# Group 0's softmax probabilities taken to their partitions by identity matmuls and ScalarE copies instead of a DMA round trip, with another hand-out order

## The chip, the cores and the metric

One NeuronCore of one Trainium2 chip. The metric is the device time of one execution in microseconds (us). TensorE is called PE, VectorE DVE, ScalarE ACT, GpSimd POOL and the queue of SyncE SP, as in the profile.

## The reference

A transformer block on one sequence of 2048 tokens with 512 features: an adaptive layer norm, sliding dilated attention, a residual, a second adaptive layer norm, a gated feed-forward part (1792 wide) and a residual.

```python
mod = silu(c) @ w_mod                       # six rows of 512: sa, ca, ga, sb, cb, gb
h = layernorm(x) * (1 + ca) + sa
q, k, v = split(h @ wqkv)                   # 32 heads of 16
off = arange(8) * 2                         # each token sees itself and 7 earlier ones, every second
logits[s, w] = q[s] . k[s - off[w]] * 16 ** -0.5    # -1e9 where s < off[w]
attn = softmax(logits, over w)
o[s] = sum_w attn[s, w] * v[s - off[w]]
x = x + ga * (o @ wo)
h = layernorm(x) * (1 + cb) + sb
x = x + gb * ((gelu(h @ w_gate) * (h @ w_up)) @ w_down)
```

## The kernel before

**Tiling.** The 2048 tokens are four groups (sg 0 to 3) of 512, each of four chunks of 128. A group goes through: `ln1` (statistics on DVE and ACT, `rstd` on POOL, normalised `x0` to `x3` on DVE), a transpose on PE or by DMA (`t1`, `transp`, L439) and its evacuation with scale and shift (`h0` to `h3` on ACT, L486); `qkv` (L543), twelve blocks `qp.sg.blk.j` of four matmuls of 128x512, evacuated by ACT as casts `qkv.sg.blk.j` (L567 to L571; blk 0 is q, 1 is k, 2 is v); the attention; `x1` (output projection and residual); `ln2`; and the feed-forward part (`g`, `u`, `gl`, `ub`, `hh`, `y`, `ot`).

**Attention.** q and k lie with features on partitions: partition 4h + d' holds head h, and j = 0 to 3 counts four slices of the 16 features. `pq.sg.j` (DVE, L616) multiplies q by the eight shifted k; `lp.sg.j` (PE, L630) sums over the features with the 0/1 matrix `M`, using the array in four quarters of 32 columns (`tile_position=(0, 32*g)`), so that the logits `LT` lie with partition = (chunk g, head) and [8 offsets, 128 tokens]. The softmax follows there (`soft`, L638): `mx` (DVE), `z` (DVE), `e` (ACT, exp), `s1`, `ri`, `p` (DVE). The result `B["e", sg]`, bf16, is kept as [w pair a, t, 128 tokens] per partition.

The second half of the attention needs the probabilities on other partitions: `PT`, one partition per (head, a), with [t, 512 tokens]. `pt_dma(sg)` (L684) does that through memory: `est.sg` stores `e` to `escr`, and `pt.sg.0`, `pt.sg.1` load it back, all on SP. The values v go through memory too: `vst.sg` stores vT, four loads `V4.sg.0` to `V4.sg.3` (L598) bring them back with two shifted rows per offset. Then `pv.sg.j` (DVE, L705) multiplies PT by V, `o.sg.j` (PE, L719) sums over the offsets with `M` in quarters again, `oT.sg.j` (ACT, L730) evacuates, and `x1p` (PE, L740) projects.

**What sets the order.** Every operation is an `Op` of a named thread (one generator each): engine, a cost in us for the planner, the function that emits it, names it comes `after`, buffers it takes and gives back, and its name `fire`. `ORDER` (L18) is a list of 872 thread numbers; the kernel emits the next operation of the thread that stands there. Each engine runs its operations in the order in which they are emitted, and waits at the head of its queue. PSUM is divided into four `mm` buffers (projection and feed-forward results), two `att` buffers (transposes, `o`, `x1`) of a bank each, and `lg`, two banks for the logits. Weights and group inputs are issued on SP in that order too, and `LN1.3.t` is a DMA transpose on SP (L454), whose result ACT evacuates as `LN1.3.h0` to `h3`.

Of the kernel before, what the change touches and what calls it, by code (L numbers as in the profile page):

```python
# [15 lines left out]
NEG = -4.0e9  # L16

ORDER = [  # L18
# [34 lines left out]
]  # L53


# [49 lines left out]
def kernel(  # L105
# [45 lines left out]

    ident = const.tile([P, P], BF16, name="ident")
    M = const.tile([P, H], BF16, name="Mph")
    maskT = const.tile([H, W, 16], F32, name="maskT")
    neghalf = const.tile([P, 4], F32, name="neghalf")
    modT = const.tile([P, 8], F32, name="modT")
# [20 lines left out]
    def setup():  # L177
        def f0():
            make_identity(nc, ident[:])
            nc.gpsimd.memset(neghalf[:], -0.5)  # L180
        yield Op("POOL", 0.9, f0, fire="ident")

        def f1():
            nc.gpsimd.memset(M[:], 1.0)
            nc.gpsimd.affine_select(out=M[:], in_=M[:], pattern=[[-4, H]], compare_op=ALU.is_ge, fill=0.0, base=0,
                                    channel_multiplier=1)
            nc.gpsimd.affine_select(out=M[:], in_=M[:], pattern=[[4, H]], compare_op=ALU.is_ge, fill=0.0, base=3,
                                    channel_multiplier=-1)
            nc.gpsimd.memset(maskT[:], 0.0)
            for w in range(1, W):  # L190
                nc.gpsimd.memset(maskT[:, W - 1 - w, 0:2 * w], NEG)
        yield Op("POOL", 2.5, f1, fire="consts")

        yield Op("POOL", 0.2, lambda: nc.gpsimd.memset(kT[:, :, 0:16], 0.0), fire="k0")

    def warmup(cold, n):
        yield Op("DVE", 0.25, lambda: nc.vector.memset(gB[:], 0.0), fire="warm")
# [386 lines left out]
    def vload(sg):  # L584
        if sg < NSG - 1:
            yield Op("POOL", 0.2, lambda: nc.gpsimd.tensor_copy(out=vh[:], in_=B["vT", sg][:, :, SG:VR]),  # L586
                     after=[f"qkv.{sg}.2.3"], fire=f"vh.{sg}")

        def f():
            nc.sync.dma_start(out=vscr[sg][:], in_=B["vT", sg][:])  # L590
        yield Op("SP", 0.65, f, after=[f"qkv.{sg}.2.3", f"vz.{sg}"], give=[SL["vs"]], fire=f"vst.{sg}", lat=1.1)
        n = 4 * VR
        for i in range(4):
            def f(i=i):
                if i == 0:
                    B["V4", sg] = T("v4", [P, 4, 4, VR], BF16, "V4")
                src = bass.AP(vscr[sg].tensor, vscr[sg].offset + i * n + 2, [[4 * n, H], [2, 4], [1, n - 8]])
                nc.sync.dma_start(out=_ap(B["V4", sg][:, i, 0, :], [[1, n - 8]]), in_=src)  # L598
            yield Op("SP", 0.65, f, after=[f"vst.{sg}"], take=[SL["v4"]] if i == 0 else [], fire=f"V4.{sg}.{i}", lat=1.6)

# [78 lines left out]
    def exp_table():  # L679
        for sg in (2, 3):  # L680
            yield Op("ACT", 0.15, lambda: nc.scalar.activation(out=junk[:], in_=neghalf[:], func=ACT.Exp), act="exp",
                     fire=f"pre.{sg}")

    def pt_dma(sg):  # L684
        def f():
            nc.sync.dma_start(out=escr[sg][:], in_=B["e", sg][:])
        yield Op("SP", 0.65, f, after=[f"p.{sg}"], give=[SL["es"]], fire=f"est.{sg}", lat=0.4)
        for t in range(2):
            def f(t=t):
                if t == 0:  # L690
                    B["PT", sg] = smp["PT"].tile([P, 2, SG], BF16, name="PT")
                src = bass.AP(escr[sg].tensor, escr[sg].offset + t * P, [[2 * P, P], [H * W * P, CPS], [1, P]])
                nc.sync.dma_start(out=B["PT", sg][:, t, :].rearrange("p (g s) -> p g s", s=P), in_=src)
            yield Op("SP", 0.65, f, after=[f"est.{sg}"] + ([f"pv.{sg - 1}.3"] if sg else []), take=[SL["PT"]] if t == 0 else [],
                     fire=f"pt.{sg}.{t}", lat=0.6)
# [14 lines left out]
    def pv_mm(sg):  # L710
        j0 = 0
        for n in GV[sg]:
            def f(j0=j0, n=n):
                for j in range(j0, j0 + n):
                    o_ps = T("att", [P, SG], F32, "o_ps")
                    B["o", sg, j] = o_ps
                    for t in range(2):
                        for i in range(4):
                            nc.tensor.matmul(o_ps[H * i:H * i + H, :], lhsT=M[:], rhs=B["pv", sg, j][:, t, i, :],  # L719
                                             start=(t == 0), stop=(t == 1), tile_position=(0, H * i))  # L720
            yield Op("PE", 0.44 * n, f, quad=True, after=[f"pv.{sg}.{j0 + n - 1}", "consts"], take=[SL["att"]] * n, give=[SL["prod"]] * n,
                     fire=f"o.{sg}.{j0 + n - 1}")
            j0 += n

# [179 lines left out]
```

## Time and profile before

| | us |
|---|---|
| Three runs | 235.75, 238.24, 236.55 |
| Median | 236.55 |
| The profiled execution's own time | 235.66 |
| Its span, first to last instruction | 233.9 |

Busy time of the profiled execution: PE 229.1 (98%), DVE 168.2 (72%), ACT 152.5 (65%), POOL 24.3 (10%). Sizes of the moved data: `escr<-e` 256 KB a store, landing 2.2 us after its issue; `PT<-escr` 128 KB a load, 3.0.

How to read it: rows of the timeline give start, length, engine, line, operation, what is written and read, and a count; in brackets stands how long the engine idled before and what it waited for. Rows of DVE and ACT overlap a little, so the price of one in a run is the distance of two starts. Rows of the stretches give busy times by engine. A shape of `128*32` for a matmul means that it uses 32 of 128 columns of the array, and four such run side by side.

### The profile page before, as it was taken

Reading aid. Unit: us, or ns where it says so; the run is one execution under the profiler, and the core shown is the slowest. Engines: PE = TensorE matmul, PEld = TensorE weight load, DVE = VectorE, ACT = ScalarE, POOL = GpSimd, SP = SyncE. Lnnn points to the kernel's source line nnn. Section 1 sums busy time; section 2 is a strip of 40 time slices with the busy share of each in tenths; the row PEclk is TensorE's granted clock in tenths of the full one; section 3 lists DMA queues with packets and bytes.
Section 4 is the critical chain, followed back from the end, with each engine's and each line's share of the span. In section 5 each row is a group of like instructions: output and inputs, shape, how many; then the busy total and the mean of one; then the engine's idle time right before and its main releaser. Section 6 shows DMA issues by size and latency. Waiting matters only on the chain.

```text
span 233.9 us, 3653 instructions
## 1 busy us (share of the span) xinstructions
PE 229.1 (98%) x1382; PEld 106.9 (46%) x1382; DVE 168.2 (72%) x240; ACT 152.5 (65%) x284; POOL 24.3 (10%) x37
## 2 busy tenths in 40 slices
PE   7899999999999999999999999999999999999995
PEld 2755454444544344444444444444444444444443
DVE  4889999999998999999899996944852213222222
ACT  4999998877997579936786961634468631467400
POOL 3210320791200000100000010000100000000000
PEclk9999999999999999999999999999999999999999
DMA  6999776999188582045003616110023000100011
GB/s 212 386 348 241 218 301 154 266 367 396 41 266 227 209 291 82 1 92 157 22 0 100 273 45 122 38 45 0 0 47 69 0 22 22 44 4 0 0 48 45
DMA packets 30217, 30.42 MB, mean 130 GB/s; under 512 B 14840, under 2 KB 26104, under 8 KB 30200
## 3 DMA queue, kind: packets, MB, share of 16 engines
q1 hardware_dynamic: 29664, 29.67, 40.8%
q10 hardware_dynamic: 536, 0.53, 0.6%
q8 instruction: 11, 0.18, 0.3%
q14 instruction: 6, 0.05, 0.1%
HBM read 22.78 MB, written 5.31 MB: 120 GB/s over the span
## 4 chain that ended last, share of the span: by engine, by line
PE 84%; DVE 9%; DMA 3%; ACT 1%; SPq 1%; issue 0%
PE g_ps L770 21%; PE u_ps L770 21%; PE y_ps L782 19%; PE qkv_ps L553 9%; PE x_ps L740 6%; DVE pq L616 5%; PE o_ps L719 3%; DMA x<-in_A_x_dram 3%; PE LTp L630 2%; PE y_ps L793 1%; DVE xn L434 1%; DVE st L394 1%; ACT qT L567 1%; DVE e L674 1%; DVE LTp L653 1%; DVE mx L647 1%
## 5 line engine op out<-in xcount | busy, mean ns | idle before, releaser
L770 PE MATMUL g_ps<-h,Wg 128*128 128x512 bf16 x224 | 57.5, 379 | 0.0
L770 PE MATMUL u_ps<-h,Wu 128*128 128x512 bf16 x224 | 57.5, 379 | 0.0
L820 DVE TENSOR_TENSOR hht<-gl,ub 128x512 bf16<-128x512 bf16 x56 | 23.0, 420 | 33.7 <-ACT ub L809 33.5
L782 PE MATMUL y_ps<-Wd,hht 128*128 128x512 bf16 x210 | 47.0, 379 | 0.0
L809 ACT CAST ub<-u_ps 128x512 bf16<-128x512 f32 x56 | 32.9, 588 | 20.4 <-PE u_ps L770 20.4
L802 ACT ACTIVATE gl<-g_ps 128x512 bf16<-128x512 f32 x56 | 33.6, 600 | 18.4 <-PE g_ps L770 16.9
L553 PE MATMUL qkv_ps<-hT,wqkv 128*128 128x512 bf16 x184 | 42.2, 380 | 0.0
L616 DVE TENSOR_TENSOR pq<-qT,kT 128x4096 bf16<-128x4096 bf16 x16 | 36.2, 2282 | 0.6 <-ACT kT L569 0.3
L705 DVE TENSOR_TENSOR pv<-PT,V 128x4096 bf16<-128x4096 bf16 x16 | 35.8, 2282 | 0.0
L770 PEld LDWEIGHTS <-Wu 128*128 128x128 bf16 x224 | 21.7, 98 | 27.0 <-issue 1.3
L770 PEld LDWEIGHTS <-Wg 128*128 128x128 bf16 x224 | 21.7, 98 | 27.0 <-issue 1.3
L782 PEld LDWEIGHTS <-hht 128*128 128x128 bf16 x210 | 20.4, 98 | 25.0 <-issue 0.4
L553 PEld LDWEIGHTS <-wqkv 128*128 128x128 bf16 x184 | 20.1, 114 | 18.5 <-issue 2.3
L425 POOL TENSOR_TENSOR rstd<-rstd,neghalf 128x4 f32<-128x4 f32 (+1 forms) x9 | 8.7, 971 | 124.4 <-DVE rstd L414 74.7
L827 DVE TENSOR_TENSOR ot<-y_ps,x 128x512 bf16<-128x512 f32 x15 | 10.1, 686 | 13.2 <-PE y_ps L782 13.2
L749 DVE TENSOR_TENSOR x<-x_ps,x 128x512 bf16<-128x512 f32 x16 | 10.7, 684 | 6.9 <-PE x_ps L740 6.9
L740 PE MATMUL x_ps<-woP,oT 128*128 128x512 bf16 x64 | 15.3, 379 | 0.0
L730 ACT CAST oT<-o_ps 128x512 bf16<-128x512 f32 x16 | 9.2, 593 | 8.7 <-PE o_ps L719 8.7
L394 DVE BATCH_NORM_STATS2 st<-x 128x6 f32<-128x512 bf16 x19 | 12.6, 680 | 2.7 <-DMA x<-in_A_x_dram 2.6
L486 ACT ACTIVATE h<-h,modT,scl 128x512 bf16<-128x512 bf16 x12 | 9.0, 809 | 7.7 <-DMA h<-xn 7.7
L586 POOL COPY vh<-vT 128x64 bf16<-128x64 bf16 x3 | 11.7, 3899 | 14.5 <-ACT vT L571 14.5
L377 ACT ACTIVATE gl<-x 128x512 bf16<-128x512 bf16 x13 | 8.3, 645 | 4.7 <-DVE x L749 3.0
(78 smaller groups left out, 189.6 us busy)
## 6 DMA issues: line engine op xcount, KB each, us to landing
V<-vscr SPq DMA_DIRECT2D x16, 526.0 KB, 6.8
wm<-in_w_mod_dram SPq DMA_DIRECT2D x5, 512.0 KB, 8.6
vscr<-vT SPq DMA_DIRECT2D x4, 528.0 KB, 9.5
out_dram<-ot SPq DMA_DIRECT2D x15, 128.0 KB, 1.7
Wg<-in_B_w_gate_dram SPq DMA_DIRECT2D x1, 1792.0 KB
Wu<-in_B_w_up_dram SPq DMA_DIRECT2D x1, 1792.0 KB
wqkv<-in_A_wqkv_dram SPq DMA_DIRECT2D x3, 512.0 KB, 7.3
x<-in_A_x_dram SPq DMA_DIRECT2D x3, 512.0 KB, 7.4
```

The lines of the kernel that those rows point to most:

```text
L394: nc.vector.bn_stats(out=k["st", c4][:], in_=src()[:, c4, :])
L553: nc.tensor.matmul(ps[:], lhsT=wqkv[blk][:, dt, j::4], rhs=B["hT", sg][:, :, dt, :], start=(dt == 0), stop=(dt == DT - 1))
L586: yield Op("POOL", 0.2, lambda: nc.gpsimd.tensor_copy(out=vh[:], in_=B["vT", sg][:, :, SG:VR]), after=[f"qkv.{sg}.2.3"], fire=f"vh.{sg}")
L616: nc.vector.tensor_tensor(out=pq[:], in0=_ap(B["qT", sg][:, j, :], [[0, W], [1, SG]]), in1=_ap(kT[:, j, sg * SG + 2:sg * SG + 2 + SG], [[2 ...
L705: nc.vector.tensor_tensor(out=t[:], in0=_ap(B["PT", sg][:, 0, :], [[SG, 2], [0, 4], [1, SG]]), in1=_ap(v[:, j, 0, :], [[8, 2], [VR, 4], [1 ...
L740: nc.tensor.matmul(ps[:], lhsT=B["oT", sg][:, j, c4 * P:(c4 + 1) * P], rhs=woP[:, j, :], start=(j == 0), stop=(j == 3))
L749: nc.vector.tensor_tensor(out=x[:, c4, :], in0=B["x1ps", sg, c4][:], in1=x[:, c4, :], op=ALU.add)
L770: nc.tensor.matmul(ps[:], lhsT=Wt[:, dt, ft * P:(ft + 1) * P], rhs=B["h2T", sg][:, :, dt, :], start=(dt == 0), stop=(dt == DT - 1))
L782: nc.tensor.matmul(ps[:], lhsT=B["hh", sg, ft][:, c4 * P:(c4 + 1) * P], rhs=B["Wd", ft // 4][:, ft % 4, :], start=(ft == 0), stop=(ft == F ...
L802: nc.scalar.activation(out=gl[:], in_=B["g", sg, ft][:], func=ACT.Gelu_apprx_tanh)
L809: nc.scalar.copy(out=ub[:], in_=B["u", sg, ft][:])
L820: nc.vector.tensor_tensor(out=hh[:], in0=B["gl", sg, ft][:], in1=B["ub", sg, ft][:], op=ALU.mult)
```

## The change

1. For group 0, `pt_dma` hands over to a new `pt_pe`: 16 matmuls on PE (`ptp.0`) with slices of the identity as the stationary side copy `e` to two PSUM banks (both `att` buffers), each of 256 columns, in four quarters; two ACT copies (`pt.0.0`, `pt.0.1`, 128x512 each) bring them to `PT`. The store and the two loads of group 0 go. The other groups are unchanged.
2. The rows of PT of group 0 then lie as (a, head) instead of (head, a): the four loads `V4.0.i` read their 128 rows in that order, and `o.0.j` uses a second 0/1 matrix `M2`, which POOL builds in five instructions (`M2`, between `vh.1` and `vz.2`).
3. `ORDER` is another list, of 873 numbers.

```diff
+    M2 = const.tile([P, H], BF16, name="Msum")
...
+        def f2():
+            nc.gpsimd.memset(M2[:], 0.0)
+            for a in range(4):
+                nc.gpsimd.affine_select(out=M2[:], in_=M2[:], pattern=[[-1, H]], compare_op=ALU.not_equal, fill=1.0,
+                                        base=-H * a, channel_multiplier=1)
+        yield Op("POOL", 1.2, f2, fire="M2")
...
-                src = bass.AP(vscr[sg].tensor, vscr[sg].offset + i * n + 2, [[4 * n, H], [2, 4], [1, n - 8]])
+                src = bass.AP(vscr[sg].tensor, vscr[sg].offset + i * n + 2, ([[4 * n, H], [2, 4]] if sg else [[2, 4], [4 * n, H]]) + [[1, n - 8]])
...
+    def pt_pe():
+        def f():
+            for h in range(2):
+                ps = T("att", [P, 2, 256], F32, "PTp")
+                B["PTp", h] = ps
+                for g in range(2):
+                    for a in range(4):
+                        nc.tensor.matmul(ps[H * a:H * a + H, :, g * P:(g + 1) * P],
+                                         lhsT=ident[:, H * (2 * h + g):H * (2 * h + g) + H],
+                                         rhs=B["e", 0][:, 2 * a:2 * a + 2, :], start=True, stop=True,
+                                         tile_position=(0, H * a))
+        yield Op("PE", 0.45, f, quad=True, after=["p.0"], take=[SL["att"]] * 2 + [SL["PT"]], give=[SL["es"]], fire="ptp.0")
+
+        for h in range(2):
+            def f(h=h):
+                if h == 0:
+                    B["PT", 0] = smp["PT"].tile([P, 2, SG], BF16, name="PT")
+                nc.scalar.copy(out=B["PT", 0][:, :, h * 256:h * 256 + 256], in_=B["PTp", h][:])
+            yield Op("ACT", 0.49, f, after=["ptp.0"], give=[SL["att"]], fire=f"pt.0.{h}")
+
     def pt_dma(sg):
+        if sg == 0:
+            yield from pt_pe()
+            return
...
-                            nc.tensor.matmul(o_ps[H * i:H * i + H, :], lhsT=M[:], rhs=B["pv", sg, j][:, t, i, :],
+                            nc.tensor.matmul(o_ps[H * i:H * i + H, :], lhsT=M[:] if sg else M2[:], rhs=B["pv", sg, j][:, t, i, :],
```

The two lists, read out as the sequence that each engine gets around the change (a line starts where both engines' lists have done the same work, but for what is shown):

```
PE before:  lp.0.0 mp2 lp.0.1 qp.1.0.0 qp.1.1.0 qp.1.2.0 lp.0.2 lp.0 qp.1.2.1 mp3 qp.1.2.2 mp4 qp.1.2.3 qp.1.0.1
            LN1.2.t0 qp.1.1.1 qp.1.0.2 qp.1.1.2 LN1.2.t1 qp.1.0.3 qp.1.1.3 lp.1.0 qp.2.0.0 qp.2.1.0 qp.2.2.0-3
            qp.2.0.1 qp.2.1.1 qp.2.0.2 o.0.0 lp.1.1 o.0.1 qp.2.1.2 qp.2.0.3 qp.2.1.3 qp.3.0.0 o.0.2 o.0.3
            qp.3.1.0 qp.3.2.0 x1p.0.0
PE after:   qp.1.0.0 lp.0.0 mp2 qp.1.1.0 qp.1.2.0 lp.0.1 mp3 lp.0.2 lp.0 qp.1.2.1 qp.1.2.2 qp.1.2.3 qp.1.0.1
            qp.1.1.1 LN1.2.t0 LN1.2.t1 qp.1.0.2 qp.1.1.2 qp.1.0.3 qp.1.1.3 ptp.0 qp.2.0.0 qp.2.1.0 qp.2.2.0-3
            qp.2.0.1 lp.1.0 o.0.0 mp4 o.0.1 qp.2.1.1 qp.2.0.2 qp.2.1.2 qp.3.0.0 qp.2.0.3 qp.2.1.3
            qp.3.1.0 o.0.2 lp.1.1 o.0.3 qp.3.2.0 x1p.0.0
DVE before: pq.0.0 x0(1.1) st0(1.2) x1-3(1.1) pq.0.1 st1(1.2) pq.0.2 pq.0.3 ... lm.0 mx.0 z.0 x0-3(1.2) s1.0 ri.0 p.0
            pq.1.0 x0(1.3) pq.1.1 x1-3(1.3) woS pv.0.0 pv.0.1 pv.0.2 pv.0.3 pq.1.2 pq.1.3 x1.0.0
DVE after:  x0-3(1.1) pq.0.0 pq.0.1 pq.0.2 st0-1(1.2) pq.0.3 ... lm.0 mx.0 z.0 x0-3(1.2) s1.0 x0(1.3) ri.0 x1(1.3) p.0
            x2-3(1.3) pq.1.0 pv.0.0 pv.0.1 pv.0.2 pv.0.3 woS pq.1.1 pq.1.2 pq.1.3 x1.0.0
ACT before: LN1.3.sq1 qkv.1.2.1 qkv.1.2.2 e.0 qkv.1.2.3 LN1.3.sq2 gc3 LN1.3.sq3 qkv.1.0.1 LN1.2.h0 qkv.1.1.1 qkv.1.0.2
            LN1.2.h1-3 gc4 qkv.1.1.2 qkv.1.0.3 qkv.2.0.0 qkv.2.1.0
ACT after:  LN1.3.sq1 qkv.1.2.1 LN1.3.sq2 qkv.1.2.2 LN1.3.sq3 e.0 qkv.1.2.3 qkv.1.0.1 LN1.2.h0 gc3 LN1.2.h1 qkv.1.1.1
            LN1.2.h2-3 qkv.1.0.2 qkv.1.1.2 pt.0.0 pt.0.1 qkv.2.0.0 pre.2 qkv.2.1.0 qkv.1.0.3
SP before:  V4.0.0 ga V4.0.1 V4.0.2 vst.1 gst3 est.0 V4.0.3 pt.0.0 pt.0.1 mc3 LN1.3.t Wg gst4 vst.2 Wu wm5 V4.1.0
SP after:   V4.0.0 V4.0.1 V4.0.2 vst.1 wm4 LN1.3.t gst3 V4.0.3 ga Wg V4.1.0 vst.2 gst4 mc3 Wu wm5
```

`x0(1.2)` stands for the normalisation of chunk 0 in LN1.2, `st` for statistics. Elsewhere the lists differ by smaller moves of the same kind: further back a few of `o`, `lp`, `x1p`, `hh`, `ot` and `WdS` change places by one or a few steps, as do evacuations and output stores.

More of the change, by code (lines that the diff above doesn't have):

```diff
@@ L718, in f @@
                         for i in range(4):
-                            nc.tensor.matmul(o_ps[H * i:H * i + H, :], lhsT=M[:], rhs=B["pv", sg, j][:, t, i, :],
+                            nc.tensor.matmul(o_ps[H * i:H * i + H, :], lhsT=M[:] if sg else M2[:], rhs=B["pv", sg, j][:, t, i, :],
                                              start=(t == 0), stop=(t == 1), tile_position=(0, H * i))
-            yield Op("PE", 0.44 * n, f, quad=True, after=[f"pv.{sg}.{j0 + n - 1}", "consts"], take=[SL["att"]] * n, give=[SL["prod"]] * n,
+            yield Op("PE", 0.44 * n, f, quad=True, after=[f"pv.{sg}.{j0 + n - 1}", "consts" if sg else "M2"], take=[SL["att"]] * n, give=[SL["prod"]] * n,
                      fire=f"o.{sg}.{j0 + n - 1}")
```

68 rows, old and new, of the table ORDER are left out of this document.

## The prediction

> Names such as `p.0` or `qp.1.0.2` are the `fire` names of the operations in the code; the order in which each engine gets them is in the section on the change.
>
> **What bounds the kernel now.** I read the busy time by stage first, then the chain that ended last, then what PE, DVE and ACT waited for in the stage of the change.
>
> ```profile
> 0.00:9.06 9.06, 7.22 (x64) 3.50 (x65) 4.71 (x16) 5.54 (x13) 3.39 (x22) 1.00 0.82 274
> 9.06:35.60 26.54, 26.27 (x218) 14.48 (x216) 25.61 (x42) 25.75 (x59) 4.78 (x7) 1.00 0.91 286
> 35.60:65.40 29.80, 29.80 (x208) 14.64 (x208) 29.51 (x32) 24.61 (x49) 12.96 (x6) 1.00 0.76 244
> ...
> 140.80:231.20 90.40, 90.38 (x455) 41.16 (x453) 35.95 (x64) 40.76 (x69) 1.01 (x1) 1.00 0.12 31
> ```
>
> After each stretch and its length stand the busy times of PE, PEld, DVE, ACT and POOL. From 9.06 us to the end PE is busy without a break, at granted clock 1.00. Until 65 us DVE is over 96% busy too, and until 35.6 us ACT with it (25.75 of 26.54). So the end is set by the sum of PE's work plus the waits of PE; an edit on another engine counts only where it makes PE wait. And a saving is small: these are PE's only waits of size between 9.06 us and the end.
>
> ```profile
> 24.34 0.62 PE L630 MATMUL LTp<-pq,Mph 128*32 128x512 bf16 x8
> 25.12 0.61 PE L630 MATMUL LTp<-pq,Mph 128*32 128x512 bf16 x8 [0.16 <-DVE pq L616]
> 25.66 1.05 PE L553 MATMUL qkv_ps<-hT,wqkv 128*128 128x512 bf16 x4
> ...
> 33.61 1.89 PE L553 MATMUL qkv_ps<-hT,wqkv 128*128 128x512 bf16 x8
> 35.60 0.62 PE L630 MATMUL LTp<-pq,Mph 128*32 128x512 bf16 x8
> ```
> ```profile
> 75.92 0.55 PE LTp L630 x8
> 76.47 0.86 PE o_ps L719 x16
> 77.33 0.97 PE g_ps L770 x4
> 78.30 0.86 PE u_ps L770 x4
> ```
>
> The second fence is from the chain that ended last and gives PE's prices: four full matmuls of 512 columns 0.86 us, sixteen on a quarter of the array each (128*32) also 0.86. Going over to quarter matmuls and back adds 0.12 (0.55 for eight instead of 0.43) and 0.11 (0.97 for the next four): 0.23 per excursion. With these, the two groups of eight from 24.34 to 25.66 need 0.97 and took 1.32, so PE waited 0.35 for `pq.0.3`; the eight full ones from 33.61 to 35.60 need 1.73 plus at most 0.11 and took 1.99, so 0.15 of waiting. Together 0.50 us: that is all that better timing can give back here.
>
> **What the change removes.** The way of the probabilities through memory: one store and two loads of group 0 on SP.
>
> ```profile
> 32.13 1.23 DVE L674 TENSOR_TENSOR e<-LTp,rinv 128x1024 bf16<-128x1024 f32 x1
> 33.27 2.28 DVE L616 TENSOR_TENSOR pq<-qT,kT 128x4096 bf16<-128x4096 bf16 x1
> ...
> 35.79 2.28 DVE L616 TENSOR_TENSOR pq<-qT,kT 128x4096 bf16<-128x4096 bf16 x1
> 38.00 1.05 DVE L434 TENSOR_SCALAR xn<-x,sums,rstd 128x512 bf16<-128x512 bf16 x3
> 38.97 1.21 DVE L360 TENSOR_TENSOR woP<-woP,gB 128x2048 bf16<-128x2048 bf16 x1
> 40.10 8.88 DVE L705 TENSOR_TENSOR pv<-PT,V 128x4096 bf16<-128x4096 bf16 x4
> ```
> ```profile
> L693 SPq DMA_DIRECT2D PT<-escr x2: 371/439/507, 35.6 to 36.0; - x2
> ...
> DMA to landing us min/median/max: 3.0/3.0/3.0
> ```
>
> The second load is issued at 36.0 and lands 3.0 later, at 39.0. DVE gets to `pv.0.0` at 40.10, and runs from `p.0` to there without idling: `pq.1.0`, `pq.1.1`, four normalisations and `woS` cover the whole way, with 1.1 us to spare. Taking it away gives 0. If the cover were gone, it would cost the 5.7 us from 33.3 to 39.0; the new order does take cover away (of these only `pq.1.0` and two normalisations stay between `p.0` and `pv.0.0`), but the rest is DVE work that comes later instead, so DVE's total does not fall.
>
> **What it adds on PE.** Sixteen quarter matmuls of 256 columns: half the columns of the sixteen `o_ps` ones, so 0.43 us. Unpacked they would take four times that, 1.73; I take 0.43, since they are placed on the four quarters in the same way. The number of excursions to quarter matmuls falls from 16 to 14 by the two lists, with `ptp.0` counted (`mp3`, `mp4` and one `lp.0` step move beside others): 2 x 0.23 = 0.46 saved; the bounds are that and 0, if a step that moves beside another still pays its switch. Sum on PE: 0.43 - 0.46 = -0.03, at worst +1.7.
>
> **What it adds elsewhere.** ACT gets two copies of 128x512, at the step of its other evacuations; POOL gets five short instructions for `M2`, a memset and four selects like this one for `M`, after `vh.1`.
>
> ```profile
> 1.63 0.21 POOL L185 TENSOR_SCALAR_AFFINE_SELECT Mph<-Mph 128x32 bf16<-128x32 bf16 x1
> ```
>
> At about 32 us that is ten us before `o.0.0` needs them, on an engine that is busy 4.78 of 26.54 us; M2 in place of M and the other row order of the V load change neither the number of matmuls nor of the 128 rows. I cost these at 0: POOL's is covered by those ten us, and would cost its 5 x 0.21 = 1.05 us if `o.0.0` came that early. `pre.2`, moved before `qkv.2.1.0`, is one short activation.
>
> **What the new order does.** Here is the cost, and it starts on ACT.
>
> ```profile
> 10.90 1.55 ACT L567 CAST qT<-qkv_ps 128x512 bf16<-128x512 f32 x3
> 12.35 0.73 ACT L383 ACTIVATE gl<-x,sums 128x512 bf16<-128x512 bf16 x1
> ...
> 14.46 0.59 ACT L567 CAST qT<-qkv_ps 128x512 bf16<-128x512 f32 x1 [0.28 <-PE qkv_ps L553]
> 15.32 0.59 ACT L569 CAST kT<-qkv_ps 128x512 bf16<-128x512 f32 x1 [0.28 <-PE qkv_ps L553]
> ```
> ```profile
> 27.36 1.23 DVE L653 TENSOR_TENSOR LTp<-LTp,mx 128x1024 f32<-128x1024 f32 x1
> ...
> 29.89 1.22 DVE L663 TENSOR_REDUCE ssum<-LTp 128x128 f32<-128x1024 f32 x1
> ...
> 31.14 0.95 DVE L669 RECIPROCAL rinv<-ssum 128x128 f32<-128x128 f32 x1
> ```
> ```profile
> 28.63 1.06 ACT L658 ACTIVATE LTp<-LTp 128x1024 f32<-128x1024 f32 x1
> ...
> 33.68 2.23 ACT L486 ACTIVATE hT<-hTp,modT,scl 128x512 bf16<-128x512 bf16 x3
> ```
>
> Start to start, a cast costs 0.48 (12.35 - 10.90 over three), a Square pass 0.72, an `hT` evacuation 0.7. Before, `e.0` began at 28.63, just as `z.0` was done. Now two more Square passes (`LN1.3.sq2`, `sq3`) stand ahead of it: 1.44 us more on an ACT that had idled only 0.56 by then, and that I expect to idle some 0.3 again. So `e.0` begins near 28.63 + 1.44 - 0.56 + 0.3 = 29.8, and ends near 30.85, while `z.0`, with the same work ahead of it on DVE as before, is ready by 29. DVE waits; then `s1.0` 1.1, `x0` 0.33, `ri.0` 1.0, `x1` 0.33, `p.0` 1.2: `p.0` is done at 34.85 instead of 33.35.
>
> PE arrives at `ptp.0` near 34.9: it did `lp.1.0` at that place at 35.60, and now `mp4` (16 of 128 columns, a quarter of 0.86) and two excursions (0.46) have gone from ahead of it, while the waits there stay at 0.5. It waits for `p.0` and for both `att` buffers, the second of which ACT frees with `LN1.2.h3`; behind `e.0` that is three casts, four `hT` and `gc3`, 4.3 us, so 35.0. `ptp.0` starts at 35.1: 0.2 of waiting, and everything behind it on PE, `qp.2.0.0` first, waits too. Ahead of it `lp.0` waits 0.25 for `pq.0.3` (25.3 instead of 25.1), and the four `mm` buffers, which ACT frees later, cost PE some 0.37 at `qp.1.0.0`, `qp.1.0.2` and `qp.2.2.0`. New waits: 0.82. Bounds: 0 if ACT keeps up, and twice that, 1.6.
>
> Then the copies: ACT does two casts and the two copies by 36.9; DVE has `x2`, `x3` and `pq.1.0` until 37.7 and finds PT there. From there DVE is full again: `pv.0`, `woS`, `pq.1.1` to `pq.1.3` (16.6 us) end at 54.25, where `x1.0.0` started at 53.31 before: 0.94 late.
>
> ```profile
> 53.31 1.28 DVE L749 TENSOR_TENSOR x<-x_ps,x 128x512 bf16<-128x512 f32 x2
> ...
> 60.66 0.72 DVE L434 TENSOR_SCALAR xn<-x,mv,rstd 128x512 bf16<-128x512 bf16 x2
> ```
> ```profile
> 61.91 1.07 PE L448 MATMUL hTp<-ident,xn 128*128 128x128 bf16 x16
> ```
> ```profile
> 70.26 0.42 DVE L820 TENSOR_TENSOR hht<-gl,ub 128x512 bf16<-128x512 bf16 x1 [0.56 <-ACT ub L809]
> 71.40 0.43 DVE L820 TENSOR_TENSOR hht<-gl,ub 128x512 bf16<-128x512 bf16 x1 [0.71 <-ACT ub L809]
> ```
>
> The normalisation of LN2.0, done at 61.4 before, is then done at 62.3; PE's transposes follow it at 61.91 before. PE's own sum gives them at 61.91 - 0.03 - 0.50 + 0.82 = 62.2, so PE waits another 0.1 there, and the feed-forward part starts 0.4 later. The rest of DVE's lateness goes into the 0.56 and 0.71 that DVE idles at 70.26 and 71.40.
>
> **SP.** Three issues leave; but `LN1.3.t`, the DMA transpose, now stands ahead of `V4.0.3`, and waits for `LN1.3.x3` on DVE.
>
> ```profile
> 33.76 0.54 SPq L598 DMA_DIRECT2D V<-vscr  x1
> ...
> 39.11 2.01 SPq L454 DMA_TRANSPOSE hT<-xn  x1
> ```
> ```profile
> DMA to landing us min/median/max: 4.4/4.4/4.4
> ```
> ```profile
> DMA to landing us min/median/max: 3.8/6.8/10.6
> ```
>
> The two rows of landings are the transpose's own and that of all sixteen V loads. `x3` is done at 35.45, the transpose is issued until 37.5, `gst3` takes half a microsecond, so `V4.0.3` goes out at 38.1 instead of 33.76. Landing in 3.8 it is there at 41.9, and `pv.0.3` starts at 44.3: covered, by 2.4 us. I take 3.8 since the transpose leaves the queues nearly empty; with the median of 6.8 it would be 0.6 late, with 10.6 4.4 late. The transpose itself lands at 39.9, when ACT gets to `LN1.3.h0`; behind that, ACT's casts free PE's buffers, and PE would wait from a landing at 41.4 on.
>
> **The sum.** 235.66 us is the profiled execution's own time (span 233.9 and 1.8 around it). 235.66 - 0.03 - 0.50 + 0.82 + 0.1 = 236.05, say 236.1. The median of the runs shown, 236.55, lies 0.9 above the profiled execution, which agrees with the fastest of them; a median of new runs should lie at or a little above the sum, and I say 236.4.
>
> **The rivals.**
> *The waits do not come* (0.24). ACT catches up, `e.0` follows `z.0`, and PE loses nothing: 235.66 - 0.03 - 0.50 = 235.1. For it: ACT had 0.56 of idling to give. Against it: 1.44 of added work ahead of `e.0`.
> *ACT's evacuation becomes the bound* (0.14). The copies cannot be covered in a stage where ACT is 97% busy, and their 0.97 us comes to PE whole through the `mm` buffers: 236.1 + 0.97 - 0.3 (the waits at `ptp.0` and LN2.0 are part of it) = 236.8. Against it: after 35.6 us ACT is busy for 24.61 of 29.80 only. The Trainium skill, TensorEngine Tiling (Array Packing), Performance Considerations, says that splitting the array speeds up TensorE but not the emptying of PSUM, which may become the bottleneck; the casts' 0.48 each against 0.43 for all sixteen matmuls agree with that, and by this rule the time would be this rival's.
> *SP's order starves DVE* (0.12), the slower side. `V4.0.3` behind the transpose lands late; it decides from 6.2 us after its issue on. Midway between median and maximum (8.7 us) it lands at 46.8, DVE idles 2.5 in front of `pv.0.3`, and nothing gives that back before LN2.0: 236.1 + 2.5 = 238.6. For it: the median of V loads. Against it: nothing large is issued ahead of it on SP after `vst.1` and `wm4`, at about 31.
> *Faster by over 1%* (0.04) would need 2.4 us, and PE has 0.5 to give after 9.06 us; only the 1.84 that PE does not work before could add to it, and that hangs on loads that keep their places.
>
> The forecast has 0.46. Range: 234.9 (waits gone, a little less) to 238.8 (V late). A measurement of this kernel can tell about 1% from no change: faster 0.06, within 1% 0.81, slower 0.13.
>
> **What would show it.** In the changed profile: `pv.0.0` starts near 37.7, behind `pq.1.0` without idling; `e.0` at 29 to 30, and DVE idle for about 0.6 ahead of `s1.0`; the `ptp.0` matmuls take 0.43 at about 35 with a short wait for DVE or ACT; first `g_ps` at 65.8 and PE unbroken after it. Wrong would be: `e.0` right behind `z.0`; a `g_ps` before 65.2 or after 66.5; an idle DVE in front of `pv.0.3`; gaps of PE after 66 us.

## The result, and the profile after

The changed kernel takes 257.08 us (median; 256.77 to 257.9), the kernel before 236.6 in the same session: ratio 1.0876, interval 1.0821 to 1.0931. The forecast was 236.4, with 238.8 as its upper end. It is 20 us slower, and the time does not come from the matmuls, the copies or the order, as the experiments show, but from a line that the prediction had costed at nothing. Ratios here and below are formed from fast executions alone; a few ran far longer for no cause in the kernel that is known (one of the kernel before 302 us, two of the first experiment, e1, 405 and 488).

The stretches of the changed kernel, with the columns as before (stretch, length, then the busy times of PE, PEld, DVE, ACT and POOL, the granted clock, the DMA engines' share and GB/s):

```profile
9.06:35.60 26.54, 26.16 (x216) 14.79 (x216) 24.49 (x45) 25.57 (x58) 5.43 (x12) 1.00 0.74 226
35.60:65.40 29.80, 17.25 (x112) 7.61 (x105) 10.84 (x5) 13.54 (x27) 1.26 (x2) 0.84 0.93 138
46.00:52.00 6.00, 4.17 (x16) 1.32 (x19) 2.08 (x1) 2.76 (x6) 1.02 (x1) 0.50 0.54 101
62.00:75.00 13.00, 5.85 (x40) 2.06 (x43) 11.10 (x7) 2.08 (x4) 1.79 (x2) 0.61 0.71 233
75.00:85.00 10.00, 10.00 (x82) 5.33 (x75) 9.50 (x18) 8.42 (x20) 1.23 (x2) 1.00 0.70 257
```

Until 35.6 us PE has lost next to nothing (26.16 us of work, 26.27 before). In the next 29.8 us PE works for 17.25 where it worked for 29.80 before, DVE for 10.84 instead of 29.51. From 75 us on PE is unbroken again. So everything is lost between some 40 and 75 us, and the chain that ended last (start, length, what) says by what:

```profile
31.65 15.44 DMA vscr<-vT
...
47.20 1.08 ACT vT L579 x2
...
48.31 0.53 SPq L305
...
48.89 14.46 DMA V<-vscr
...
66.90 2.21 DVE pq L624
...
69.15 1.04 PE LTp L638 x8
```

Two transfers of half a megabyte take 15.4 and 14.5 us. The first is the store of group 1's `vT` (`vst.1`), the second the fourth V load of group 0 (`V4.0.3`). Before, the trace has the same store land 4.7 us after its issue and the same load 3.8.

Here is what waited for them; first PE, then DVE, ACT and SP, each with the idle time in brackets:

```profile
35.19 0.69 PE L699 MATMUL PTp<-e,ident 128*32 128x256 bf16 x16
...
47.83 3.57 PE L561 MATMUL qkv_ps<-hT,wqkv 128*128 128x512 bf16 x8 [7.19 <-ACT vT L579]
...
69.15 1.04 PE L638 MATMUL LTp<-pq,Mph 128*32 128x512 bf16 x8 [8.98 <-DVE pq L624]
```
```profile
31.11 1.22 DVE L671 TENSOR_REDUCE ssum<-LTp 128x128 f32<-128x1024 f32 x1 [0.71 <-ACT LTp L666]
...
33.67 1.21 DVE L682 TENSOR_TENSOR e<-LTp,rinv 128x1024 bf16<-128x1024 f32 x1
...
37.65 2.28 DVE L737 TENSOR_TENSOR pv<-PT,V 128x4096 bf16<-128x4096 bf16 x1
40.70 2.29 DVE L737 TENSOR_TENSOR pv<-PT,V 128x4096 bf16<-128x4096 bf16 x1 [0.78 <-DMA V<-vscr]
45.78 2.29 DVE L737 TENSOR_TENSOR pv<-PT,V 128x4096 bf16<-128x4096 bf16 x1 [2.79 <-DMA V<-vscr]
63.47 2.29 DVE L737 TENSOR_TENSOR pv<-PT,V 128x4096 bf16<-128x4096 bf16 x1 [15.39 <-DMA V<-vscr]
```
```profile
47.20 1.07 ACT L579 CAST vT<-qkv_ps 128x512 bf16<-128x512 f32 x2 [8.25 <-DMA vscr<-vT]
50.31 0.81 ACT L494 ACTIVATE hT<-hT,modT,scl 128x512 bf16<-128x512 bf16 x1 [2.04 <-DMA hT<-xn]
```
```profile
31.65 0.34 SPq L598 DMA_DIRECT2D vscr<-vT  x1
...
35.59 12.66 SPq L462 DMA_TRANSPOSE hT<-xn  x1
```

PE's two waits are 16.2 us. The span grew by 21.2 (255.1 against 233.9); the other 5 are mostly the clock: after 7 us without work PE runs at a granted clock of 0.50 (stretch 46 to 52), and eight full matmuls take 3.57 us where eight took 1.89 before. The second wait has the same behind it (the 0.61 of the stretch from 62 to 75 is a mean). The issue of the transpose held SP's queue for 12.66 us (2.01 before), and behind it stood `V4.0.3`, which so went out at 48.89.

Why are the transfers slow? The DMA share and the GB/s between 24.5 and 35 us, in 40 slices, first before, then after:

```profile
DMA  2000945999999843689989999999998731200996
GB/s 87 23 8 0 175 96 160 401 353 401 420 252 212 119 75 116 147 196 355 337 321 401 385 401 385 433 401 418 402 450 341 290 145 80 97 33 32 391 398 226
```
```profile
DMA  0000010513023221022132222132236999995989
GB/s 0 0 4 0 0 31 0 111 80 112 32 80 112 80 64 64 16 96 96 80 112 64 80 96 80 64 128 96 95 112 241 434 370 338 402 305 155 269 268 287
```

After, until `vst.1` joins in, the sixteen DMA engines are mostly busy to one to three tenths (four of sixteen at full work would give two and a half), and they move about 100 GB/s, where before they moved up to 450. The landing events of the trace say the same: of each V load of before there are sixteen, between 27.6 and 28.3 us for the first one; of each load of the changed kernel five, one about 1 us after its issue and four later (34.8, 40.7 and 45.8 us for the last of the first three loads). The store `vst.1` behind them, issued at 31.65, shows both groups of engines at once: of its sixteen events twelve come at 34.4 to 34.6 us and four at 45.3 to 47.1.

### The profile page after: what moved, and what is told of

Read it like the earlier page. It is cut to its first block, busy times and chain, and to the rows that moved or that the text cites. A ratio compares the mean times of both kernels' runs of the same rounds, so it can differ in the third digit from the quotient of the medians.

```text
span 255.1 us, 3686 instructions
## 1 busy us (share of the span) xinstructions
PE 233.8 (92%) x1398; PEld 108.2 (42%) x1398; DVE 168.1 (66%) x240; ACT 150.0 (59%) x284; POOL 16.2 (6%) x42
## 4 chain that ended last, share of the span: by engine, by line
PE 73%; DMA 15%; ACT 7%; DVE 2%; issue 1%; SPq 1%; DVEq 0%; ACTq 0%; POOLq 0%
PE g_ps L802 19%; PE u_ps L802 19%; PE y_ps L814 18%; DMA vscr<-vT 6%; DMA V<-vscr 6%; PE x_ps L772 5%; PE qkv_ps L561 5%; DMA wqkv<-in_A_wqkv_dram 3%; PE o_ps L751 3%; PE LTp L638 2%; ACT vT L579 2%; ACT gl L391 1%; PE y_ps L825 1%; ACT gl L385 1%; ACT hT L494 1%
## 5 line engine op out<-in xcount | busy, mean ns | idle before, releaser
L561 PE MATMUL qkv_ps<-hT,wqkv 128*128 128x512 bf16 x184 | 44.8, 396 | 7.7 <-ACT vT L579 7.4
L561 PEld LDWEIGHTS <-wqkv 128*128 128x128 bf16 x184 | 20.7, 116 | 28.6 <-issue 12.4
L638 PE MATMUL LTp<-pq,Mph 128*32 128x512 bf16 x128 | 9.6, 411 | 9.0 <-DVE pq L624 9.0
L579 ACT CAST vT<-qkv_ps 128x512 bf16<-128x512 f32 x16 | 9.4, 620 | 9.5 <-DMA vscr<-vT 8.2
```

The source lines that it names most:

```text
L561: nc.tensor.matmul(ps[:], lhsT=wqkv[blk][:, dt, j::4], rhs=B["hT", sg][:, :, dt, :], start=(dt == 0), stop=(dt == DT - 1))
L579: nc.scalar.copy(out=B["vT", sg][:, j, VH:], in_=ps[:])
L638: nc.tensor.matmul(B["LT", sg][H * g:H * g + H, 4 * t:4 * t + 4, :], lhsT=M[:], rhs=B["pq", sg, j][:, 4 * t:4 * t + 4, g * P:(g + 1) * P], ...
```

## The theories

Theory A: the new row order of group 0's V loads, with 4 as its slowest dimension in place of 32, confines each of them to 4 of 16 DMA engines; three of them stand there for some 20 us, and every later transfer that uses all sixteen lands behind them on these four. It makes V late for DVE, `vT`'s buffer late for ACT and the transpose late for ACT and SP. Its rivals: B, SP's order alone (the rival of the prediction); C, the order of the rows in memory, whichever engines bring them; and that the rest of the change has a gain that V hides.

## The experiments

**The row order alone.** First the old rows in the changed kernel (e1), then the new rows in the kernel before (e2), then the new rows in the changed kernel, brought by four loads each (e3).

```diff
-                src = bass.AP(vscr[sg].tensor, vscr[sg].offset + i * n + 2, ([[4 * n, H], [2, 4]] if sg else [[2, 4], [4 * n, H]]) + [[1, n - 8]])
+                src = bass.AP(vscr[sg].tensor, vscr[sg].offset + i * n + 2, [[4 * n, H], [2, 4]] + [[1, n - 8]])
```

> The changed kernel with group 0's four V loads reading their rows as before, (head, a), and all else kept: the identity matmuls, the copies, M2, the order. V then stands on other partitions than PT, so group 0's attention is not the reference's. Theory A (the new row order puts each V load on 4 of the 16 DMA engines, because the slowest dimension of its source is now 4; they take 5.3 us each there and hold up whatever comes behind them on those engines): the V loads land as before, about 4 us after issue, nothing waits, 236.1 us as the blind sum had it, within 1.5. Rival B (SP's order, with the transpose ahead of the fourth V load, starves DVE whatever the rows): over 245. Rival C (reading the scratch in a-major order is slow in memory, not on the engines): 236 here as well.

Measured: ratio 1.003 (0.9984 to 1.0076), the profiled execution 236.90 us. DVE no longer idles in front of `pv`, the loads land 3.9 to 7.1 us after their issue, and the feed-forward part begins at 66.10 us (65.40 before, 65.8 forecast). The first row is of DVE, the second the landings of the first three V loads (the fourth takes 3.9), the third of PE:

```profile
37.70 8.88 DVE L737 TENSOR_TENSOR pv<-PT,V 128x4096 bf16<-128x4096 bf16 x4
```
```profile
DMA to landing us min/median/max: 3.9/6.5/7.1
```
```profile
66.10 1.03 PE L802 MATMUL g_ps<-h,Wg 128*128 128x512 bf16 x4
```

So everything but the row order is worth +0.7 us at the start of the feed-forward part, and B is out: SP's order is in this kernel as it was.

```diff
-                src = bass.AP(vscr[sg].tensor, vscr[sg].offset + i * n + 2, [[4 * n, H], [2, 4], [1, n - 8]])
+                src = bass.AP(vscr[sg].tensor, vscr[sg].offset + i * n + 2, ([[4 * n, H], [2, 4]] if sg else [[2, 4], [4 * n, H]]) + [[1, n - 8]])
```

> The kernel before with only the new row order in group 0's V loads (again the rows of V do not match PT's in group 0). Theory A: each of the first three loads takes about 5.3 us after the other, landing near 34, 40 and 45, the store of group 1's v waits behind them, PE waits for its evacuations, the fourth load lands near 51: 245 to 252 us. Rival B: 236.6, since SP's order is that of before. Rival C: as theory A in time, but with the rows on all 16 engines.

Measured for e2: 250.69 us (median of two executions, 248.87 and 252.5), ratio 1.0549 (1.0388 to 1.071). The loads land at 36.98, 42.47, 47.60 and 55.18, five events each. In the chain that ended last now stand the store and the load of the probabilities that the change was to remove, and PE has one long wait:

```profile
36.04 13.53 DMA escr<-e
...
50.00 5.95 DMA PT<-escr
```
```profile
49.52 9.70 PE L553 MATMUL qkv_ps<-hT,wqkv 128*128 128x512 bf16 x36 [10.64 <-ACT gR L348]
```

The row order alone makes the kernel before some 14 us slower; any transfer behind it pays, here a quarter-megabyte store with 13.5 us in place of 2.2.

```diff
-                nc.sync.dma_start(out=_ap(B["V4", sg][:, i, 0, :], [[1, n - 8]]), in_=src)
...
+                    for a in range(4):
+                        src = bass.AP(vscr[0].tensor, vscr[0].offset + i * n + 2 + 2 * a, [[4 * n, H], [1, n - 8]])
+                        nc.sync.dma_start(out=_ap(B["V4", 0][H * a:H * a + H, i, 0, :], [[1, n - 8]]), in_=src)
```

> The changed kernel with each of group 0's four V loads issued as four loads of 32 rows, one for each a; the same rows are read in the same a-major order to the same partitions, but the slowest dimension of each is 32. Theory A: each piece goes over 16 engines again, 236 to 238 us (twelve more issues on SP, about 0.6 us each, mostly where SP waits anyway). Rival C (a-major reading is slow): over 250, like the changed kernel.

Measured: the profiled execution 237.44 us, ratio 1.0136 (0.998 to 1.0291), too wide to tell it from no change (all four executions lie between 237.4 and 243.3), but far from 257. All sixteen pieces show sixteen landing events. The same rows of memory reach the same partitions as in the changed kernel, only with 32 as the slowest dimension: C falls.

**How many engines.** If the slowest dimension sets the number, 8 (e4) gives a part of the loss and 16 (e5) none.

```diff
-                src = bass.AP(vscr[sg].tensor, vscr[sg].offset + i * n + 2, ([[4 * n, H], [2, 4]] if sg else [[2, 4], [4 * n, H]]) + [[1, n - 8]])
+                src = bass.AP(vscr[sg].tensor, vscr[sg].offset + i * n + 2, ([[4 * n, H], [2, 4]] if sg else [[2, 8], [8 * n, 16]]) + [[1, n - 8]])
```

> The changed kernel with group 0's V loads reading 8 shifts of 16 rows (content not the reference's for group 0), slowest dimension 8. Theory A: 8 of the 16 engines, 16 rows each, so about 2.6 us a load instead of 5.3; the first three land near 30, 32 and 35, the fourth about 5 us after its issue; PE is not held up by them. 236 to 243 us: the upper end if the halo copy of group 2 on POOL, which waits for the store behind these loads, starts after DVE's long row of multiplies and is held until it ends (theory D, from the run with slowest dimension 16, where that copy took 18.8 us and a weight load behind it came 2.9 us late). Rival C: over 250.

> The changed kernel with group 0's V loads reading 16 shifts of 8 rows, slowest dimension 16, one load each of the same size (V's content is then not the reference's for group 0). Theory A: 16 engines, as fast as with the rows of before, 236 us within 1.5. Rival C: overlapping rows read shift by shift, so over 250.

e5 has `[[2, 16], [16 * n, 8]]` at that place. With 8, nine landing events a load; the first three land at 31.17, 37.00 and 39.62, the fourth at 50.01, and the time is 245.15 us, ratio 1.0388 (1.0231 to 1.0544). That is 2 us over the range expected of it. V is late here too: DVE idles 5.8 us in front of `pv.0.3`. With 16, sixteen events a load, and they land nearly as early as the old rows (4.5 to 8.3 us after their issue); but the time is 244.14, ratio 1.0274 (1.0131 to 1.0416), 6.6 us over what was expected, and within the noise the same as with 8. The number of engines explains the landings, then, and not this time. The mean share of the DMA engines from 26.0 to 31.6 us agrees with the landings: 0.23 in the changed kernel, 0.51 with 8, 0.87 with the old rows of e1. What explains the time with 16 stands in its waits and its POOL: in the waits of PE a late `wm`, and in the timeline of POOL a copy of 128x64, in e1 0.24 us long. The first row is the landings of its first three V loads:

```profile
DMA to landing us min/median/max: 4.5/7.4/8.3
```
```profile
PE gR_ps L351 <- DMA wm<-in_w_mod_dram: 2.9, 1, 2.9
```
```profile
35.55 18.84 POOL L587 COPY vT<-vh 128x64 bf16<-128x64 bf16 x1 [2.24 <-DMA vscr<-vT]
```
```profile
35.46 2.28 DVE L624 TENSOR_TENSOR pq<-qT,kT 128x4096 bf16<-128x4096 bf16 x1
37.66 8.89 DVE L737 TENSOR_TENSOR pv<-PT,V 128x4096 bf16<-128x4096 bf16 x4
46.47 1.22 DVE L368 TENSOR_TENSOR woP<-woP,gB 128x2048 bf16<-128x2048 bf16 x1
47.61 6.68 DVE L624 TENSOR_TENSOR pq<-qT,kT 128x4096 bf16<-128x4096 bf16 x3
```

The copy begins 0.09 us after DVE has begun a run of nine multiplies with both inputs in SBUF, and ends at 54.39, 0.1 after the run's end. The store `vst.2` on SP waits for this copy and goes out at 54.41 (47.24 in e1), and behind it the loads of `Wu` and `wm`. PE waits 2.9 us for `wm`, and behind that runs at a granted clock of 0.50 (65 to 70 us), where twelve full matmuls take 4.66 us instead of 2.75; together the feed-forward part begins 5.8 us later than in e1. This is theory D, a side effect of when the copy begins. In e3 the copy met the run as well, and was let go in the run's only gap, where DVE idles:

```profile
35.62 11.08 POOL L587 COPY vT<-vh 128x64 bf16<-128x64 bf16 x1 [2.26 <-DMA vscr<-vT]
```
```profile
47.20 1.23 DVE L368 TENSOR_TENSOR woP<-woP,gB 128x2048 bf16<-128x2048 bf16 x1 [0.60 <-DMA gB<-gscr]
```

To test theory D, the copy was to begin earlier: two buffers for `vs`, so that it need not wait for `vst.1` (and three for `q`, for the room; otherwise as e5).

```diff
-    NB = {"x": 4, "hT": 2, "xn": 2, "q": 4, "vs": 1, "v4": 1, "prod": 4, "ot4": 1, "h2": 2,
+    NB = {"x": 4, "hT": 2, "xn": 2, "q": 3, "vs": 2, "v4": 1, "prod": 4, "ot4": 1, "h2": 2,
```

> The run with slowest dimension 16 again, with two buffers for vT instead of one (and three for q instead of four, to make room), so that group 2's halo copy on POOL does not wait for group 1's store and runs before DVE's long row of multiplies. Theory D (that run's extra came from the copy being held while DVE multiplied): the copy takes under 1 us near 33 and the time is 236 to 238.5. If the shift-by-shift reading itself cost the extra (rival C in small): 242 to 245 again.

Measured: 238.55 us, at the upper end of what was expected, ratio 1.0064 (1.0013 to 1.0115); the copy takes 0.24 at 35.13, ahead of DVE's run, which in this execution starts at 37.34 (its first stage took 1.9 us longer). Theory D holds, and sixteen engines cost what the old rows cost.

**Which of the loads, and which way to PE.** Here are one part of the row order each (e7, e6), the other order of SP (e8), and the changed kernel with two buffers for `vs` (e9). Their edits are a condition on `i` in the line above, `V4.0.3` put ahead of `LN1.3.t` in the list, and the `NB` line.

> The changed kernel with the new row order in the first three V loads of group 0 only, the fourth as before. Theory A: the three still land near 35, 40 and 46, group 1's store near 47, ACT and PE wait for it as in the changed kernel, the transpose is issued until 48 and the fourth load goes out at 48.9, but lands within about 5 us, near 54, instead of 63.4: 257 less about 9, so 246 to 250 us. If only the fourth load mattered (rival B): 237.

> The changed kernel with only the fourth load of group 0's V in the new row order and the first three in the old one (so that group 0's attention output is not the reference's). Theory A: the fourth is issued at 38.7 onto engines that are free but for the transpose; on 4 of them its 128 rows take 5.3 us at least, so it lands at 44 to 48, where pv.0.3 would start at 44.3: PE loses 0 to 3, 237 to 241. With the 251 of the run with only the first three new, nearly all of the loss is then theirs. If the fourth load itself is what decides (DVE's wait for it was the longest, 15.4 us), 246 to 257.

The first three alone: 250.92 us (one run). The fourth alone: 249.45 (one run), and that is a miss, 237 to 241 had been expected. The first stages of these two executions took some 2.5 us longer (`vst.0` goes out at 24.5 and 24.2 us, against 21.8), so they stand for 248 and 247. The chain of each (the first row of each fence) and what PE waited for:

```profile
34.34 15.16 DMA vscr<-vT
```
```profile
PE qkv_ps L561 <- ACT vT L579: 7.6, 3, 6.9
```
```profile
41.07 13.71 DMA V<-vscr
```
```profile
60.59 1.04 PE L638 MATMUL LTp<-pq,Mph 128*32 128x512 bf16 x8 [7.45 <-DVE pq L624]
```

The rows of the changed kernel's chain return one by one: the store goes with the first three loads, the long `V<-vscr` with the fourth. I had thought the fourth alone on its four engines, with the 5.1 to 5.9 us that the second and third of the changed kernel needed for 32 rows an engine; but 1.1 us behind it SP issues the load of `Wg`, 1.8 MB on all sixteen. Of the sixteen events of `Wg`, twelve come at 54.9 to 56.2 us and four at 59.0 to 59.3, and the V load lands at 54.8: so the four engines worked on both. The changed kernel's 14.46 stand beside `Wg` too. The two halves cost 11 and 10 us over e1's 236.9, and together 20.

> The changed kernel, all new rows, with the fourth V load of group 0 put ahead of the transpose on SP. Theory A: the fourth load queues behind the other three on the same four engines and lands near 52; group 1's store still lands near 47, and the transpose behind all of them: 245 to 252 us, part of the loss only. Rival B: 237.

Measured: 254.1 us (one run), 2 us over the range expected, as much as its first stage is longer. With `V4.0.3` ahead of the transpose the load lands at 55.63 and the transpose at 57.43: one of the two always waits for the engines. SP's order is not the cause.

> The changed kernel with its new row order, but two buffers for vs (three instead of four for q). Theory A says that the loss has two ways to PE: through vT, which waits for the buffer of vst.1's store (7 to 8 us of PE's waits and the slow clock behind them), and through pv, which waits for V (9 us at LTp). This takes the first away and leaves the second: 245 to 252, with vT not waiting and PE not waiting for qkv before 50 us, and pv still waiting 10 to 20. If vst.1 alone were the way, 236 to 239; if its buffer had nothing to do with it, 256 to 258.

Measured: 256.68 us (one run). That is a miss, 245 to 252 had been expected, and the value that was to be seen if the buffer had nothing to do with the loss. PE no longer waits for `vT`, but as long at the next place. Of its ACT and of the waits of its PE:

```profile
50.39 0.81 ACT L494 ACTIVATE hT<-hT,modT,scl 128x512 bf16<-128x512 bf16 x1 [9.58 <-DMA hT<-xn]
```
```profile
PE gR_ps L351 <- ACT kT L577: 8.0, 1, 8.0
```

ACT comes to `hT` with no stop at `vT`, and waits there for the transpose, which lands at 50.37 as in the changed kernel (50.29). Taking one dependent away gives nothing, since store and transpose both stand behind the three loads and land 3 us apart (47.2 and 50.4).

**The change as it was meant (e11).** Four pieces per load, and two `vs` buffers, so that neither the engines nor the POOL copy disturb.

> The changed kernel with each of group 0's four V loads as four loads of 32 rows (the computation is the reference's), and with two buffers for vs instead of one (and three instead of four for q, to make room), so that nothing of group 0's V is late and vst.1 holds up neither ACT's vT nor POOL's halo copies. If V's way was the whole of the loss, and the rest of the change is worth what the run with the old rows showed (+0.7 us by its profile), 236.3 (235.3 to 237.8). The rival, that the change's own gain was hidden by V all along, gives 233 to 235. A POOL copy that meets DVE's long run of multiplies again would show as a wait of PE for wm, and some 3 to 8 us more.

Measured: 237.43 us against 236.7, ratio 1.0028 (0.9994 to 1.0062), the profiled execution 236.73. This is within 1% and rather slower than faster; the feed-forward part begins at 66.15 us, 0.75 later than before. No version here beats the kernel before.

## Why the prediction was wrong

**The step that failed** is half a sentence in what the change adds elsewhere: "M2 in place of M and the other row order of the V load change neither the number of matmuls nor of the 128 rows. I cost these at 0". The 128 rows and their bytes are the same; what changed is how they are dealt out to the DMA engines. e1 and e2 show the price, 20 us with the rest of the change and 14 without it, and the changed kernel, e4, e5 and e3 show the reason: landing events of 4, 8 and 16 engines for a slowest dimension of 4, 8, and 16 or 32, whatever the order of the rows. The Trainium skill, DMA: Bandwidth & Descriptors, section "Why a DMA increments its semaphore by 16 and not by 1", has the rule: the number of engines is the largest up to 16 that divides the slowest dimension (other than 1) on both sides of the transfer, and the issuing sequencer itself posts the rest of the sixteen completions at once. The five and nine events of the traces agree with both halves of it: one about 1 us after the issue, then four or eight.

**The duration taken for `V4.0.3`.** The prediction took 3.8 us, "since the transpose leaves the queues nearly empty", with 6.8 and 10.6 as bounds from rows of before. It was 14.46. All three had come from sixteen-engine loads, so no row of before could bound it. (The row with 3.8, 6.8 and 10.6 covers only the ten V loads of sixteen whose landing the view pairs, and `V4.0.3` is not one of them; its own events of before end 3.8 us after its issue as well.) In e1, where the load has sixteen engines, it took 3.9: the choice was right for the kernel that the prediction had in mind.

**The rival of the slower side** (SP's order starves DVE, 238.6) named the place, an idle DVE in front of `pv.0.3`, and the wrong mechanism: with the same order and old rows there is no wait at all (e1), and with the other order the loss stays (e8). The rival of ACT's evacuation (236.8) is close to the 236.90 of e1 by luck: it wanted 0.97 us through the `mm` buffers, and PE waits for ACT 0.23 us there.

**What held.** "The DMA round trip is covered": e1 and e11 show no gain from taking it away. `p.0` was forecast to be done at 34.85 (34.88 in the rows above), DVE's idling ahead of `s1.0` at 0.6 (0.71), `ptp.0` at 35.1 (35.19), `pv.0.0` at 37.7 right behind `pq.1.0` (37.65). The sum without the row order was +0.4 at the start of the feed-forward part; e1 shows +0.70, e11 +0.75. Of its new waits, the one at `lp.0` for `pq.0.3` did not come (its sixteen matmuls run in 1.03 us at 25.10 in e1), and of the 0.37 for `mm` buffers 0.23 came, at `qp.1.0.2`, behind ACT's `vT` (31.70 in e1). The 0.3 that the sum lacks show at the new step: in e1 `ptp.0` starts at 35.24, 0.14 later than forecast, and 0.76 us pass from there to the next matmul (36.00), where 0.43 and a switch of 0.12 had been costed. Why it takes that long was not followed up.

## What to carry to other kernels

When an edit reorders the dimensions of a DMA, bytes and rows do not give its price: look at the slowest dimension, since 4 and 8 there gave four and eight engines, and 16 and 32 all sixteen. A small one is repaired by cutting the transfer along it (e3, e11). In a profile it shows as a DMA share stuck at k sixteenths while nothing else is in flight (0.23 here for 4, 0.51 for 8). And the slow transfer is not where the loss appears: look at everything issued after it, since a transfer over all engines lands with its slowest share.

## What the runs showed of the hardware

- A DMA transpose behind busy engines holds its queue: its issue took 12.66 us on SP in the changed kernel against 2.01 before, and all that SP issues later moved with it.
- A half-megabyte store over all engines landed after 15.4 us instead of 4.7 because 4 of its 16 shares stood behind other rows: twelve shares landed by 34.6 us, the other four at 45.3 to 47.1.
- A POOL copy of 128x64, 0.24 us alone, takes as long as DVE's run of multiplies from two SBUF inputs still lasts when it begins: 18.84 us in e5. Each of these copies ended 0.1 us after the run did, also where the run ended in an idle DVE (11.08 us in e3, 3.43 in e4). The kernel before has it too, and PE does not wait there. Here is the row of before:

```profile
42.27 11.22 POOL L586 COPY vh<-vT 128x64 bf16<-128x64 bf16 x1 [6.63 <-ACT vT L571]
```

The Trainium skill, SBUF — State Buffer, section "Who interferes with whom", says that a `tensor_tensor` with both inputs in SBUF contends with GpSimd's reads, that such contention is an exclusive lock, and that the order of issue decides who is blocked. The traces agree, with the addition that a run of nine instructions without a gap (e5) counted as one.
- PE that had stood idle for 7.2 us came back at a granted clock of 0.50 (46 to 52 us of the changed kernel), and eight full matmuls took 3.57 us instead of 1.89; after 2.9 us (e5, 65 to 70 us) it was 0.50 too, and even after 2.4 us (e4) eight quarter matmuls took 0.81 us from start to start (55.81 to 56.62) where they take 0.44 elsewhere.
